# DVE and ACT in written order from tile 72 on, in a fused attention and feed-forward kernel

## The chip, the cores and the metric

The kernel runs on one core of one Trainium2 chip. The metric is the device time of one execution in microseconds; the time before is the median of three runs, 1441.31 us (1440.77 to 1443.91).

## The reference

Attention runs over 8 batches of 8 heads, 576 positions, 64 numbers each, in float32. A score counts if it is at least the row's maximum less tau; softmax goes over the scores that are left. The result is laid out as 4608 tokens of 512 numbers and goes through a feed-forward network (FFN) with 2048 hidden numbers and softplus between its two products. What is computed, cut to its core:

```python
scores = scale * np.matmul(q, k.transpose(0, 1, 3, 2))
thresh = np.max(scores, axis=-1, keepdims=True) - tau
scores = np.where(scores >= thresh, scores, -1000000000.0)
attn = np.exp(scores - np.max(scores, axis=-1, keepdims=True))
attn = attn / (np.sum(attn, axis=-1, keepdims=True) + 1e-09)
x = np.matmul(attn, v).transpose(0, 2, 1, 3).reshape(B * S, H * D)
h = x @ w_in
g = np.maximum(h, 0.0) + np.log1p(np.exp(-np.abs(h)))
out = g @ w_out
```

## The kernel before

**Attention.** The work is cut into 32 units, a batch and a pair of heads each, and a unit into 9 tiles of 128 rows (the fifth tile holds the last 64 rows of both heads): 288 tiles. Names carry the unit and the tile, so negm_10_7 is the maximum of tile 7 of unit 10, which is tile 97 of the kernel. Tile 72 is the first of unit 8. Products run on PE in a format that keeps fewer bits, so operands are split into a hi part and a lo part that is what hi leaves over. For a tile, PE computes scores into one of two PSUM banks (s_0 and s_1, L423); DVE reduces them to the negated row maximum (negm, L430) and sets the threshold (thr, L431); ACT takes the exponential into e_all (L435); DVE masks it and sums its rows (L440). PE then transposes the weights, into the score bank that they came from (L471, L474); ACT copies them out as hi (gH, L498, L503, L510) and DVE makes the lo part (gL, and the corrections in gH, both L132). Only when lo is done may the bank take the scores of the tile two places on. PE multiplies the weights with v (pv, L555 to L557); ACT and DVE add the halves into xp (L565, L566). At a unit's end DVE turns the row sums into factors (rs, L571, L572), which go to POOL by way of memory; POOL scales xp (L593), and SP stores it to x_d.

**FFN.** Tokens come in 9 chunks of 512. A chunk's x is loaded in four quarters (xst, SP, L613); ACT makes xh (L127) and POOL xl (L132). PE makes 16 hidden blocks of 12 matmuls (h, L645 to L649), ACT takes softplus of two blocks at a time (st, L667), DVE casts to hi (g0, L129) and POOL makes lo (g1, L132). PE projects in 4 groups of 4 hidden blocks for 4 blocks of tokens (o, L713; o_1_1_0 is chunk 1, group 1, tokens 0); the sum is kept in acc, set by ACT for the first group (L727) and added to by DVE afterwards (L729). Softplus and the exponential need different tables on ACT, so each change of function has an ACT_TABLE_LOAD.

**The order.** Attention and FFN are woven: the tile loop goes through the letters of `PAT = "ThRlefmpfxSvwp"`. T is the transposes of a tile's weights, h the hi copies, R the reduce of the next tile, l the lo parts, e and m exp and mask of the next tile, S the scores of the tile two places on. Each f lets PE take half of the tile's share of FFN matmuls. Each p is a point at which deferred work is written: softplus, casts of g, the adds into acc, copies of transposed q and k. A chunk's x is split while the chunk before it is projected for the last time; the last quarter is written where the last of these projections ends, right ahead of the chunk's first hidden block.

This written order is not the order that runs. Instructions are handed to a scheduler, which sets the order in each engine's queue by priorities and by estimates of when operands are there. Softplus has a raised priority (`SPP = 150`). Each engine then takes its own queue in that order. Four PSUM banks (tag g) go round among h, o, pv and transposed q and k. Two helpers write order down: `behind(i, others)` makes instruction i come after the last of others in a queue without a wait on a semaphore, and is used for a few instructions only.

Chunk 0 to 6 begin with attention still running; the rest of the FFN comes after the last tile, from about 1240 us.

Of the kernel before, what the change touches and what calls it, by code (L numbers as in the profile page):

```python
# [51 lines left out]
NF = 5  # L52
TG = 36
# [6 lines left out]
def tile_kernel(ctx: ExitStack, tc: tile.TileContext, q, k, v, tau, w_in, w_out, out):  # L60
# [62 lines left out]
    def hi_of(eng, out_, in_):  # L123
        if eng is nc.gpsimd:
            eng.tensor_scalar(out=out_, in0=in_, scalar1=1.0, scalar2=1.0, op0=ALU.mult, op1=ALU.mult)
        elif eng is nc.scalar:
            eng.copy(out_, in_)  # L127
        else:
            eng.tensor_copy(out_, in_)  # L129
# [20 lines left out]
    def to_f32(src, want, name, then):  # L150
# [41 lines left out]
        def first():  # L192
            nc.scalar.activation(m, high.bitcast(F32), AF.Abs, scale=2.0 ** 16)
            nc.gpsimd.tensor_scalar(out=m, in0=m, scalar1=W_MAX, scalar2=W_MIN, op0=ALU.min, op1=ALU.max)
            later_(1, lambda: second(0))


        def second(n):
            if n == 0:
                i = nc.vector.tensor_scalar(out=mu, in0=mu, scalar1=3, scalar2=None, op0=ALU.logical_shift_left)  # L200
            elif n == 1:
                i = nc.vector.scalar_tensor_tensor(out=mu, in0=high, scalar=0x80000000, in1=mu,
                                                   op0=ALU.bitwise_and, op1=ALU.bitwise_or)
            else:
                i = nc.vector.scalar_tensor_tensor(out=mu, in0=low, scalar=29, in1=mu,
                                                   op0=ALU.logical_shift_right, op1=ALU.bitwise_or)
# [68 lines left out]
    for b in range(B):  # L275
        for kind in (("one", "two") if b < NSPLIT else ("all",)):
            for hp in range(NPAIR):
# [14 lines left out]
                s.eng = (nc.gpsimd, nc.scalar)[SPA] if b < NSPLIT else nc.gpsimd  # L292
# [58 lines left out]
    def qkT(s, j, n):  # L351
# [13 lines left out]
        if n == 0:  # L365
            s.kT.append(apool.tile([P, S + SR], F32R, tag="kT", name=f"kT_{s.i}_{j}"))
            t = s.kT[j]
            defer(1, lambda: nc.scalar.copy(t[:, SR:S], ps))
# [6 lines left out]
    def queries(s, t0, t1, ps):  # L375

        nc.scalar.activation(t0, ps, AF.Copy, scale=qscale)
# [3 lines left out]
        for i, o in ((slice(0, D), slice(D, P)), (slice(D, P), slice(0, D))):  # L381
            nc.vector.tensor_scalar(out=t1[o], in0=ps[i], scalar1=qscale[i], scalar2=None, op0=ALU.mult)
# [5 lines left out]
    def qkT_rest(s, j, ps):  # L388

        nc.scalar.copy(  # L390
# [3 lines left out]
        if j == 0 and s.kind != "one":  # L394
            for m in range(2):
                nc.scalar.activation(qm[:, 0, m, m * SR:(m + 1) * SR], ps[:, P + m * SR:P + (m + 1) * SR],
                                     AF.Copy, scale=qscale)
# [29 lines left out]
    def row_max(s, t):  # L427
        negm = apool.tile([P, 1], F32, tag="negm", bufs=3, name=f"negm_{s.i}_{t}")
        thr = apool.tile([P, 1], F32, tag="thr", bufs=3, name=f"thr_{s.i}_{t}")
        nc.vector.reduce_max(negm, s.sp[t][:, :, 0:HS], axis=AX.XY, negate=True)  # L430
        nc.vector.tensor_scalar(out=thr, in0=negm, scalar1=-1.0, scalar2=ntau, op0=ALU.mult, op1=ALU.add)  # L431
        s.m[t] = (negm, thr)

    def exps(s, t):
        nc.scalar.activation(e_all[:, s.half[t], :].rearrange("p (h n) -> p h n", h=2), s.sp[t][:, :, 0:HS],  # L435
                             AF.Exp, bias=s.m[t][0], scale=1.0)

    def mask(s, t):
        e2 = e_all[:, s.half[t], :].rearrange("p (h n) -> p h n", h=2)
        masked.append(nc.vector.scalar_tensor_tensor(  # L440
# [52 lines left out]
    def weights_hi(s, t):  # L493
        main, rest = s.sp[t]
        for g, c0, s0, n in s.place[t]:
            h = group(s, g)[0]
            h = h.bitcast(F32) if s.whole else h
            nc.scalar.copy(h[:, 0:NC, c0:c0 + n], main[:, :, s0:s0 + n])  # L498
        both = rests(s, t)
        if len(both) == 2 and not s.whole:  # L500

            (g, c0, _, n), = s.place[both[0][0]]
            nc.scalar.copy(group(s, g)[0][:, NC, c0:c0 + 2 * n].rearrange("p (k n) -> p k n", k=2),  # L503
                           rest.unsqueeze(1).to_broadcast([P, 2, n]))
            return
        for x, rows, up, down in both:
            for g, c0, s0, n in s.place[x]:
                h = group(s, g)[0][:, NC, c0:c0 + n]
                if not s.whole:
                    nc.scalar.copy(h[up], rest[rows, s0:s0 + n])  # L510
                elif len(both) == 2:
                    nc.scalar.activation(h.bitcast(F32), rest, AF.Copy, scale=side[:, s.half[x]:s.half[x] + 1])  # L512
                else:
                    nc.scalar.copy(h[up].bitcast(F32), rest[rows, s0:s0 + n])
                    nc.gpsimd.memset(h[down].bitcast(F32), 0.0)

    def weights_lo(s, t):
# [3 lines left out]
        for g, c0, s0, n in s.place[t]:  # L521
            h, l = group(s, g)
            lo_of(nc.vector, l[:, :, c0:c0 + n], main[:, :, s0:s0 + n], h[:, 0:NC, c0:c0 + n])
        for x, rows, up, down in rests(s, t):
            for g, c0, s0, n in s.place[x]:
                h = group(s, g)[0]
                lo_of(nc.vector, h[down, NC, c0:c0 + n], rest[rows, s0:s0 + n], h[up, NC, c0:c0 + n])
# [14 lines left out]
    def values(s, g):  # L542
# [5 lines left out]
        if s.whole:  # L548
            slow.append([lambda c=c: nc.tensor.matmul(o[0:D, 0:n], s.vn[:, 5 * j + c, :], h[:, c, 0:n].bitcast(F32),  # L549
                                                      start=(c == 0), stop=(c == NC)) for c in range(NC + 1)])  # L550
            ends.append(lambda: nc.scalar.copy(s.xp[j * D:(j + 1) * D, x0:x0 + n], o[0:D, 0:n]))  # L551
# [8 lines left out]
    def values_out(s, g, o):  # L560
# [4 lines left out]
        nc.scalar.copy(xs, o[move, 0:n])  # L565
        nc.vector.tensor_tensor(out=xs, in0=o[keep, 0:n], in1=xs, op=ALU.add)  # L566

    def row_scales(s):
        nt = len(s.tiles)
        s.rs = apool.tile([P, 9], F32, tag="rs", name=f"rs_{s.i}")  # L570
        nc.vector.tensor_scalar(out=s.rs[:, 0:nt], in0=s.sums[:, 0:nt], scalar1=1e-9, scalar2=None, op0=ALU.add)  # L571
        nc.vector.reciprocal(s.rs[:, 0:nt], s.rs[:, 0:nt])  # L572
# [6 lines left out]
    def row_scales_out(s, ps):  # L579
        nt, n = len(s.tiles), s.n  # L580
        rt = apool.tile([P, S], F32, tag="R", bufs=1, name=f"rt_{s.i}")[0:9, 0:P]
        nc.scalar.copy(rt[0:nt, :], ps[0:nt, 0:P])
# [33 lines left out]
    def split_x(u, cc):  # L616
# [6 lines left out]
        hi_of(nc.scalar, u.h[cc], st)  # L623
# [36 lines left out]
    def softplus(u, full):  # L660
# [3 lines left out]
        with tc.high_priority(SPP):  # L664
            for fc, bank in reversed(full):
                t = fpool.tile([P, TC], F32, tag="st", bufs=NST, name=f"st_{u.n}_{fc}")
                i = nc.scalar.activation(t, bank, AF.Softplus).ins  # L667
# [16 lines left out]
    def parts_of(u, fc, t):  # L684
# [10 lines left out]
        hi_of(nc.vector if u.n else nc.scalar, gh, t)  # L695
# [25 lines left out]
    def project_out(u, qt, tb, o):  # L721
# [4 lines left out]
        if qt == 0:  # L726
            nc.scalar.copy(a, o)  # L727
        else:
            nc.vector.tensor_tensor(out=a, in0=o, in1=a, op=ALU.add)  # L729
# [78 lines left out]
    now = {"p": 0}  # L808
# [114 lines left out]
    eng, u0.eng, u0.eng_lo = u0.eng, nc.scalar, nc.vector  # L923
# [21 lines left out]
    for g, (cur, t) in enumerate(tiles):  # L945
        t9 = cur.tiles.index(t) + 1
# [73 lines left out]
```

## Time and profile before

| | |
|---|---|
| median of 3 runs | 1441.31 us (1440.77 to 1443.91) |
| the profiled execution | 1442.01 us |
| its span, first to last instruction | 1440.2 us |
| mean granted clock of PE | 1.000 |
| PE busy | 1392.3 us, 97% of the span |
| DVE busy | 990.8 us, 69% |
| ACT busy | 850.9 us, 59% |
| POOL busy | 591.0 us, 41% |
| DMA | 189.93 MB, mean 132 GB/s |

Rows of a time line read: start, length, engine, line, operation, out<-in, shapes, count; in brackets the idle time just before on that engine and what ended it. PE rows overlap: a matmul of 512 columns is shown about 0.4 us long, while the next one starts sooner than that. A row of a group reads: line, engine, operation and shapes, count, then busy time and the mean in ns, then the engine's idle time ahead of the group and what ended most of it.

### The profile page before, as it was taken

What the parts mean: (1) busy time and instruction counts of PE and PEld (TensorE: products, weight loads), DVE (VectorE), ACT (ScalarE), POOL (GpSimd) and SP (SyncE); (2) the same over time, 40 slices, a digit from 0 to 9 for tenths busy, and PEclk for the clock granted to TensorE, in tenths of its full rate; (3) what the DMA queues carried; (4) which work ended last, traced back from release to release, by engine and by line L of the source; (5) the groups of instructions that cost most, each with busy time, mean ns of one, the idle gap of its engine ahead of it and who ended that gap; (6) DMA issues with size and microseconds to landing.
All of it is one profiled execution on the core that took longest, in us unless ns stands there. A gap on an engine that the chain in (4) does not pass through costs nothing.

```text
span 1440.2 us, 23512 instructions
## 1 busy us (share of the span) xinstructions
PE 1392.3 (97%) x7860; PEld 1160.7 (81%) x7860; DVE 990.8 (69%) x2211; ACT 850.9 (59%) x1615; POOL 591.0 (41%) x619
## 2 busy tenths in 40 slices
PE   6887899999999999999999999999999999999998
PEld 5555688788888888888888888888888888788886
DVE  6888688787777777777777777777777777402112
ACT  5776777667666576667666665757666765311010
POOL 3676666543334333344334333444334431324221
PEclk9999999999999999999999999999999999999999
DMA  5767766445334534345433533454344532333321
GB/s 156 220 190 206 228 200 184 127 122 160 98 102 119 137 110 124 117 136 152 118 109 107 149 109 99 126 145 121 114 119 139 150 95 83 105 123 126 121 85 44
DMA packets 131208, 189.93 MB, mean 132 GB/s; under 512 B 35312, under 2 KB 86800, under 8 KB 131088
## 3 DMA queue, kind: packets, MB, share of 16 engines
q1 hardware_dynamic: 131088, 188.43, 44.8%
q8 instruction: 63, 1.03, 0.3%
q14 instruction: 57, 0.47, 0.1%
HBM read 140.51 MB, written 27.41 MB: 117 GB/s over the span
## 4 chain that ended last, share of the span: by engine, by line
PE 80%; DVE 8%; ACT 4%; issue 4%; POOL 2%; DMA 1%; SPq 1%; POOLq 0%; DVEq 0%; ACTq 0%
PE o L713 24%; PE s L423 11%; PE h L645 9%; PE h L647 9%; PE h L649 8%; PE s L474 7%; PE pv L555 3%; PE pv L556 3%; DVE e_all L440 2%; PE tr L364 2%; DVE negm L430 1%; ACT L667 1%; PE pv L549 1%; ACT st L667 1%; PE s L471 1%
## 5 line engine op out<-in xcount | busy, mean ns | idle before, releaser
L713 PE MATMUL o<-wo_o,g 128*128 128x512 f32 x1728 | 449.8, 400 | 1.1 <-POOL g L132 1.1
L713 PEld LDWEIGHTS o<-wo_o,g 128*128 128x128 f32 x1728 | 313.4, 188 | 59.9 <-POOL g L132 2.1
L132 POOL TENSOR_TENSOR g<-st,g 128x512 fp32r<-128x512 f32 x144 | 191.5, 1347 | 194.0 <-DVE g L129 180.0
L440 DVE SCALAR_TENSOR_TENSOR e_all<-s,thr,e_all 128x576 f32<-128x576 f32 x288 | 234.1, 815 | 48.8 <-ACT e_all L435 45.3
L430 DVE TENSOR_REDUCE negm<-s 128x1 f32<-128x576 f32 x288 | 216.9, 753 | 37.7 <-PE s L423 30.8
L435 ACT ACTIVATE e_all<-s,negm 128x576 f32<-128x576 f32 x288 | 215.6, 749 | 37.8 <-DVE negm L430 18.6
L645 PE MATMUL h<-xh,wi 128*128 128x512 f32 x576 | 231.3, 402 | 2.1 <-ACT xp L551 0.8
L647 PE MATMUL h<-xl,wi 128*128 128x512 f32 x576 | 232.2, 403 | 0.7 <-POOL xl L132 0.7
L649 PE MATMUL h<-xh,wi 128*128 128x512 f32 x576 | 229.7, 399 | 0.0
L498 ACT CAST gH<-s 128x512 fp32r<-128x512 f32 (+1 forms) x270 | 144.8, 549 | 133.8 <-PE s L474 130.7
L132 DVE TENSOR_TENSOR gL<-s,gH 128x512 fp32r<-128x512 f32 (+1 forms) x270 | 168.9, 634 | 58.1 <-ACT gH L498 31.7
L423 PE MATMUL s<-kT,qT 128*128 128x288 f32 x1024 | 193.0, 310 | 7.8 <-ACT gH L512 2.0
L423 PEld LDWEIGHTS s<-kT,qT 128*128 128x128 f32 x1024 | 148.2, 190 | 29.1 <-issue 9.6
L129 DVE CAST g<-st 128x512 fp32r<-128x512 f32 x128 | 63.0, 529 | 147.9 <-ACT st L667 147.4
L474 PE MATMUL s<-identr,e_all 128*128 128x128 f32 x1008 | 153.6, 275 | 4.0 <-DVE e_all L440 3.9
L667 ACT ACTIVATE st<-h 128x512 f32<-128x512 f32 x144 | 78.3, 596 | 115.6 <-PE h L649 115.1
L474 PEld LDWEIGHTS s<-identr,e_all 128*128 128x128 f32 x1008 | 115.0, 140 | 20.1 <-DVE e_all L440 12.5
L645 PEld LDWEIGHTS h<-xh,wi 128*128 128x128 f32 x576 | 108.4, 188 | 25.7 <-ACT xh L127 1.3
L647 PEld LDWEIGHTS h<-xl,wi 128*128 128x128 f32 x576 | 108.4, 188 | 22.3 <-POOL xl L132 1.4
L649 PEld LDWEIGHTS h<-xh,wi 128*128 128x128 f32 x576 | 108.3, 188 | 22.0
L555 PE MATMUL pv<-gH,vt 128*128 128x256 f32 (+1 forms) x432 | 118.8, 297 | 0.4 <-ACT gH L498 0.4
L556 PE MATMUL pv<-gL,vt 128*128 128x256 f32 (+1 forms) x432 | 118.8, 296 | 0.0
(103 smaller groups left out, 1911.2 us busy)
## 6 DMA issues: line engine op xcount, KB each, us to landing
wi<-wi_d SPq DMA_DIRECT2D x144, 512.0 KB
qT<-qT SPq DMA_DIRECT2D x124, 128.0 KB
R<-r_d SPq DMA_DIRECT2D x64, 144.0 KB
kn<-in_k_dram SPq DMA_DIRECT2D x32, 256.0 KB
qn<-in_q_dram SPq DMA_DIRECT2D x32, 256.0 KB
vn<-in_v_dram SPq DMA_DIRECT2D x32, 256.0 KB
wc_i<-in_moe_w_in_dram SPq DMA_DIRECT2D x16, 512.0 KB
wi_d<-wc_i SPq DMA_DIRECT2D x32, 256.0 KB
```

What stands on the lines that cost most here:

```text
L132: eng.tensor_tensor(out=out_, in0=in_, in1=hi.bitcast(F32), op=ALU.subtract)
L423: i = nc.tensor.matmul(sp[:, hf, 0:HS], lhs, s.kT[j][:, k0 + hf * HS:k0 + (hf + 1) * HS], start=(m == 0), stop=(m == len(parts) - 1))
L430: nc.vector.reduce_max(negm, s.sp[t][:, :, 0:HS], axis=AX.XY, negate=True)
L435: nc.scalar.activation(e_all[:, s.half[t], :].rearrange("p (h n) -> p h n", h=2), s.sp[t][:, :, 0:HS], AF.Exp, bias=s.m[t][0], scale=1.0)
L440: masked.append(nc.vector.scalar_tensor_tensor(out=e2, in0=s.sp[t][:, :, 0:HS], scalar=s.m.pop(t)[1], in1=e2, op0=ALU.is_ge, op1=ALU.mult, ...
L474: nc.tensor.matmul(main[:, c, :], e[:, c0:c0 + P], ident, is_transpose=True, start=True, stop=True)
L555: nc.tensor.matmul(o[:, 0:n], vt[:, c, :], h[:, c, 0:n], start=(c == 0), stop=False)
L556: nc.tensor.matmul(o[:, 0:n], vt[:, c, :], l[:, c, 0:n], start=False, stop=False)
L645: nc.tensor.matmul(h, wi[:, 0, cc, :], u.h[cc], start=(cc == 0), stop=False)
L647: nc.tensor.matmul(h, wi[:, 0, cc, :], u.l[cc], start=False, stop=False)
L649: nc.tensor.matmul(h, wi[:, 1, cc, :], u.h[cc], start=False, stop=(cc == NCC - 1))
L713: nc.tensor.matmul(o, u.g[fc][m // 2][:, sl], wo[fc][:, m % 2, :], start=(n == 0), stop=(n == 3 * QF - 1))
```

## The change

A class `Queue` stands in for DVE (`vec`) and for ACT (`act`) wherever the kernel writes an instruction to them. From tile 72 on, and through all that follows the last tile, it puts each instruction behind the one written before it on the same engine. What is written, and where, stays as it was, and so do the tiles and the buffers. PE, POOL and SP are still ordered by the scheduler, whose estimates see the new order of the other two.

```diff
+TQ = 72
...
+    now = {"p": 0, "tile": 0}
...
+    class Queue:
+
+        def __init__(self, eng):
+            self.eng, self.last = eng, []
+
+        def __getattr__(self, name):
+            def call(*args, **kwargs):
+                i = getattr(self.eng, name)(*args, **kwargs)
+                if now["tile"] >= TQ:
+                    behind(i, self.last)
+                    self.last = [i]
+                return i
+            return call
+
+    vec = Queue(nc.vector)
+    act = Queue(nc.scalar)
...
-        nc.vector.reduce_max(negm, s.sp[t][:, :, 0:HS], axis=AX.XY, negate=True)
+        vec.reduce_max(negm, s.sp[t][:, :, 0:HS], axis=AX.XY, negate=True)
...
-            nc.vector.tensor_tensor(out=a, in0=o, in1=a, op=ALU.add)
+            vec.tensor_tensor(out=a, in0=o, in1=a, op=ALU.add)
...
     for g, (cur, t) in enumerate(tiles):
+        now["tile"] = g
```

Every other `nc.vector` and `nc.scalar` of the loop is replaced in the same way. In the changed kernel all instructions of DVE and ACT carry one line, L156, that of the call in `Queue`.

DVE's queue at the seam of units 10 and 11, before; s_1 is a score bank, acc_1_0 the sum of chunk 1:

```order
L729 TENSOR_TENSOR acc_1_0_4271<-o_1_1_0_4647,acc_1_0_4271 128x512
L440 SCALAR_TENSOR_TENSOR e_all_141,sums_10_4307<-s_1_143,thr_10_7_4690,e_all_141 128x576
L430 TENSOR_REDUCE negm_10_8_4741<-s_0_142 128x1
L431 TENSOR_SCALAR thr_10_8_4742<-negm_10_8_4741,ntau_85 128x1
L132 TENSOR_TENSOR gL_10_3_4739<-s_1_143,gH_10_3_4738 128x4x128
L440 SCALAR_TENSOR_TENSOR e_all_141,sums_10_4307<-s_0_142,thr_10_8_4742,e_all_141 128x576
L571 TENSOR_SCALAR rs_10_4801<-sums_10_4307 128x9
L572 RECIPROCAL rs_10_4801<-rs_10_4801 128x9
L566 TENSOR_TENSOR xp_10_4481<-pv_10_2_4754,xp_10_4481 64x320
L430 TENSOR_REDUCE negm_11_0_4778<-s_1_143 128x1
L729 TENSOR_TENSOR acc_1_0_4271<-o_1_1_1_4706,acc_1_0_4271 128x512
L431 TENSOR_SCALAR thr_11_0_4779<-negm_11_0_4778,ntau_85 128x1
```

The same queue at the same place in the changed kernel:

```order
L156 SCALAR_TENSOR_TENSOR e_all_141,sums_10_4307<-s_1_143,thr_10_7_4690,e_all_141 128x576
L156 TENSOR_TENSOR acc_1_0_4271<-o_1_1_0_4647,acc_1_0_4271 128x512
L156 TENSOR_REDUCE negm_10_8_4741<-s_0_142 128x1
L156 TENSOR_SCALAR thr_10_8_4742<-negm_10_8_4741,ntau_85 128x1
L156 TENSOR_TENSOR gL_10_3_4739<-s_1_143,gH_10_3_4738 128x4x128
L156 SCALAR_TENSOR_TENSOR e_all_141,sums_10_4307<-s_0_142,thr_10_8_4742,e_all_141 128x576
L156 TENSOR_TENSOR xp_10_4481<-pv_10_2_4754,xp_10_4481 64x320
L156 TENSOR_REDUCE negm_11_0_4778<-s_1_143 128x1
L156 TENSOR_SCALAR thr_11_0_4779<-negm_11_0_4778,ntau_85 128x1
L156 TENSOR_TENSOR gL_10_3_4739<-s_0_142,gH_10_3_4738 128x4x128
L156 TENSOR_TENSOR gH_10_3_4738<-s_0_142,gH_10_3_4738 64x128 x2
L156 SCALAR_TENSOR_TENSOR e_all_141,sums_11_4764<-s_1_143,thr_11_0_4779,e_all_141 128x576
```

The add of o_1_1_0 has changed places with the mask of tile 10_7. The add of o_1_1_1 and the two instructions for rs_10 have gone behind the mask of tile 11_0, which is the last row here; they are the next three, and the reduce of tile 11_1 follows them.

ACT's queue ahead of chunk 2, before; xst_2_3 is the last quarter of that chunk's x, and PE reads it in unit 13:

```order
L390 CAST kT_13_0_5466<-tr_13_0_2_5517 128x2x64
L396 ACTIVATE qm_107<-tr_13_0_2_5517,qscale_88 128x64 x2
L377 ACTIVATE qT0_13_0_5525<-tr_13_0_1_5520,qscale_88 128x512
L127 CAST xh_2_2_5620<-xst_2_3_5564 128x512
L498 CAST gH_12_2_5478<-s_1_143 128x4x128
L435 ACTIVATE e_all_141<-s_0_142,negm_12_6_5549 128x576
```

The same queue in the changed kernel, where that instruction now stands:

```order
L156 CAST gH_12_3_5656<-s_0_142 128x4x128
L156 CAST gH_12_3_5656<-s_0_142 128x256
L156 ACTIVATE e_all_141<-s_1_143,negm_13_0_5698 128x576
L156 CAST xh_2_2_5620<-xst_2_3_5564 128x512
L156 CAST kT_13_1_5635<-tr_13_1_2_5732 128x2x64
L156 CAST gH_13_0_5757<-s_1_143 128x4x128
```

The cast of the last quarter has moved from ahead of the exp of tile 12_6 to behind that of tile 13_0. On POOL its lo part moved along, to behind the first split of q for unit 14 (q2_14_0). On PE the one matmul of h_2_0 that reads the last quarter's lo part has gone behind the transpose of tr_13_1_2 and one score matmul.

ACT's queue in unit 13, the first of chunk 2, before:

```order
L503 CAST gH_13_0_5757<-s_0_142 128x256
L667 ACT_TABLE_LOAD
L667 ACTIVATE st_2_1_5821<-h_2_1_5769 128x512
L667 ACTIVATE st_2_0_5823<-h_2_0_5715 128x512
L435 ACT_TABLE_LOAD
L435 ACTIVATE e_all_141<-s_1_143,negm_13_2_5803 128x576
L582 COPY rt_12_5848<-rT_12_5831 9x128
L435 ACTIVATE e_all_141<-s_0_142,negm_13_3_5861 128x576
```

And in the changed kernel:

```order
L156 CAST gH_13_0_5757<-s_0_142 128x256
L156 ACTIVATE e_all_141<-s_1_143,negm_13_2_5803 128x576
L156 ACT_TABLE_LOAD
L156 ACTIVATE st_2_1_5821<-h_2_1_5769 128x512
L156 ACTIVATE st_2_0_5823<-h_2_0_5715 128x512
L156 COPY rt_12_5848<-rT_12_5831 9x128
L156 CAST gH_13_1_5858<-s_1_143 128x4x128
L156 ACT_TABLE_LOAD
L156 ACTIVATE e_all_141<-s_0_142,negm_13_3_5861 128x576
```

The pair of softplus with its table load has changed places with the exp of tile 13_2, and the exp of tile 13_3 has come behind the hi copy of tile 13_1. Two more pairs of the unit, ahead of the exps of tiles 13_4 and 13_6, move in the same way. The number of instructions is the same on every engine, and so is that of table loads. In the first units of the other chunks the rows change as in unit 13; in the three units behind it the pairs of softplus stay where they were.

More of the change, by code (lines that the diff above doesn't have):

```diff
@@ L564, in values_out @@
         xs = s.xp[keep, x0:x0 + n]
-        nc.scalar.copy(xs, o[move, 0:n])
-        nc.vector.tensor_tensor(out=xs, in0=o[keep, 0:n], in1=xs, op=ALU.add)
+        act.copy(xs, o[move, 0:n])
+        vec.tensor_tensor(out=xs, in0=o[keep, 0:n], in1=xs, op=ALU.add)
     def row_scales(s):
@@ L666, in softplus @@
                 t = fpool.tile([P, TC], F32, tag="st", bufs=NST, name=f"st_{u.n}_{fc}")
-                i = nc.scalar.activation(t, bank, AF.Softplus).ins
+                i = act.activation(t, bank, AF.Softplus).ins
                 if last_ is not None:
@@ L807, in tile_kernel @@
     later = []
-    now = {"p": 0}
     def defer(n, f):
```

58 lines of the change are left out of this document (29 added, 29 removed).

## The prediction

> **What bounds the kernel now.** I read the page's engine totals first, then the busy time by stretches of the span, then the groups by line, and last the time line of PE, DVE and ACT around PE's waits.
>
> ```profile
> PE 1392.3 (97%) x7860; PEld 1160.7 (81%) x7860; DVE 990.8 (69%) x2211; ACT 850.9 (59%) x1615; POOL 591.0 (41%) x619
> PE   6887899999999999999999999999999999999998
> ```
>
> PE has work for 97% of the span, and the slices show that what it lacks lies almost wholly in the first fifth, which the change leaves as it is. The stretches (columns: PE, PEld, DVE, ACT and POOL busy, clock, DMA share) say how much is left where the change acts, from tile 72, about 297 us:
>
> ```profile
> 297.00:1240.00 943.00, 937.64 (x5564) 808.52 (x5562) 720.91 (x1651) 619.30 (x1147) 357.80 (x370) 1.00 0.42 120
> 1240.00:1440.20 200.20, 194.82 (x840) 157.31 (x839) 34.88 (x63) 29.24 (x51) 57.47 (x43) 1.00 0.35 108
> ```
>
> In those 943 us PE is idle for 943.00 - 937.64 = 5.4 us by the records. DVE is busy 76% and ACT 66%: neither is a bound, and their order can only matter through PE's few waits. Records of waits start after the overlapped end of the last matmul, so I measure a wait by how far two matmuls start apart, against their undisturbed distance. The groups by line name the wait that is worth most:
>
> ```profile
> L474 PE MATMUL s<-identr,e_all 128*128 128x128 f32 x1008 | 153.6, 275 | 4.0 <-DVE e_all L440 3.9
> L713 PE MATMUL o<-wo_o,g 128*128 128x512 f32 x1728 | 449.8, 400 | 1.1 <-POOL g L132 1.1
> ```
>
> The transposes of the weights wait 3.9 us for the mask. The time line shows where, on PE, at the seam of units 10 and 11; the later rows are the last place of the same kind:
>
> ```profile
> 401.40 0.46 PE L364 MATMUL tr<-identr,k 128*128 128x128 f32 x4
> 401.69 0.51 PE L364 MATMUL tr<-identr,q 128*128 128x128 f32 x4
> 402.03 0.77 PE L423 MATMUL s<-kT,qT 128*128 128x288 f32 x4
> 402.64 0.40 PE L713 MATMUL o<-wo_o,g 128*128 128x512 f32 x1
> 403.37 0.66 PE L474 MATMUL s<-identr,e_all 128*128 128x128 f32 x4 [0.34 <-DVE e_all L440]
> ...
> 407.34 3.00 PE L713 MATMUL o<-wo_o,g 128*128 128x512 f32 x12
> 410.18 0.22 PE L356 MATMUL tr<-identr,k 128*128 128x128 f32 x1
> 410.47 0.76 PE L423 MATMUL s<-kT,qT 128*128 128x288 f32 x4
> ...
> 1190.92 0.66 PE L474 MATMUL s<-identr,e_all 128*128 128x128 f32 x4 [0.33 <-DVE e_all L440]
> ```
>
> Twelve o matmuls and the step to the next instruction take 410.18 - 407.34 = 2.84 us, 0.235 each. The transposes of 403.37 start 0.73 after the o of 402.64, so they lose 0.73 - 0.235 = 0.5 us. At a third of a microsecond of recorded idle each, 3.9 us are 11 to 12 such places; I count 11 in PE's time line, at two seams of every four units. A second, unrecorded loss follows 7 us later: after one transpose (0.29 / 4 = 0.07 each, from the row of 401.40) the scores start 0.29 later, so 0.22 is lost; this too comes 11 times.
>
> DVE's rows at the two places show why:
>
> ```profile
> 401.27 0.59 DVE L132 TENSOR_TENSOR gH<-s,gH 64x128 fp32r<-64x128 f32 x2
> 401.89 0.69 DVE L729 TENSOR_TENSOR acc<-o,acc 128x512 f32<-128x512 f32 x1
> 402.49 0.81 DVE L440 SCALAR_TENSOR_TENSOR e_all<-s,thr,e_all 128x576 f32<-128x576 f32 x1
> 403.23 0.75 DVE L430 TENSOR_REDUCE negm<-s 128x1 f32<-128x576 f32 x1
> ...
> 407.52 0.76 DVE L430 TENSOR_REDUCE negm<-s 128x1 f32<-128x576 f32 x1
> 408.31 0.69 DVE L729 TENSOR_TENSOR acc<-o,acc 128x512 f32<-128x512 f32 x1
> 409.04 0.68 DVE L132 TENSOR_TENSOR gL<-s,gH 128x512 fp32r<-128x512 f32 x1
> 409.74 0.59 DVE L132 TENSOR_TENSOR gH<-s,gH 64x128 fp32r<-64x128 f32 x2
> 411.27 0.76 DVE L430 TENSOR_REDUCE negm<-s 128x1 f32<-128x576 f32 x1
> ```
>
> At each place an add of the FFN into acc, which PE does not need soon, stands ahead of what PE waits for: ahead of the mask at 402.49, and ahead of the gL and gH at 409.04, the last readers of the score bank that the scores of 410.47 overwrite.
>
> ACT around the same places, with a softplus between its two table loads ahead of the first:
>
> ```profile
> 395.60 1.28 ACT L667 ACT_TABLE_LOAD   x1
> 396.89 1.09 ACT L667 ACTIVATE st<-h 128x512 f32<-128x512 f32 x2
> 398.60 0.59 ACT L498 CAST gH<-s 128x512 fp32r<-128x512 f32 x1 [0.18 <-PE s L474]
> 399.48 1.28 ACT L435 ACT_TABLE_LOAD   x1
> 400.78 0.74 ACT L435 ACTIVATE e_all<-s,negm 128x576 f32<-128x576 f32 x1
> 404.54 0.75 ACT L435 ACTIVATE e_all<-s,negm 128x576 f32<-128x576 f32 x1
> ...
> 412.43 0.75 ACT L435 ACTIVATE e_all<-s,negm 128x576 f32<-128x576 f32 x1
> ```
>
> **The change part by part. The mask.** In the written order the add stands behind the mask. The mask then starts when gH ends, about 401.86, and ends at 402.67; PE, which is now given one more o first, wants it at 402.64 + 2 x 0.235 = 403.11. So 0.44 us are to spare and the whole 0.5 goes: 11 x 0.5 = 5.5 us. The add now stands ahead of the reduce of 403.23 instead, but the mask has left its place 0.6 earlier, so the reduce starts when it did. Its exp stands at 404.54 behind a hi copy, 0.56 after the reduce ends, so that is covered.
>
> **The lo parts.** With the add gone from 408.31, gL follows the hi copy and ends, with gH, about 0.6 us earlier; the scores want the bank 0.5 earlier (the gain above) and no longer wait: 11 x 0.22 = 2.4 us. What is late next is the reduce of 411.27: behind it now stand the add (0.69) and the two small row-scale instructions, about 0.4 together. Counted from PE's scores it starts 0.4 later, and its exp, which stood at 412.43 behind a hi copy, 0.40 after the reduce's end, has just that much cover. I take nothing, with 0.2 x 11 = 2.2 us as the bad end.
>
> **The first x split of a chunk.** These rows are ACT, POOL and PE at the start of chunk 2:
>
> ```profile
> 474.60 0.62 ACT L127 CAST xh<-xst 128x512 fp32r<-128x512 f32 x1 [1.60 <-DMA xst<-x_d]
> 487.27 0.76 ACT L435 ACTIVATE e_all<-s,negm 128x576 f32<-128x576 f32 x1
> ...
> 475.30 1.29 POOL L132 TENSOR_TENSOR xl<-xst,xh 128x512 fp32r<-128x512 f32 x1 [1.93 <-ACT xh L127]
> 482.70 0.46 POOL L125 TENSOR_SCALAR q<-qn 128x320 fp32r<-128x320 f32 x1 [4.74 <-PE s L474]
> 483.24 0.88 POOL L132 TENSOR_TENSOR q<-qn,q 128x320 fp32r<-128x320 f32 x1
> 489.43 0.68 POOL L125 TENSOR_SCALAR k<-kn 128x576 fp32r<-128x576 f32 x1 [5.31 <-PE tr L356]
> ...
> 488.89 0.39 PE L647 MATMUL h<-xl,wi 128*128 128x512 f32 x1
> 489.12 0.22 PE L356 MATMUL tr<-identr,k 128*128 128x128 f32 x1
> 489.38 0.76 PE L423 MATMUL s<-kT,qT 128*128 128x288 f32 x4
> ```
>
> Now the last xl is done at 476.59, 12 us before the matmul of 488.89 reads it. In the written order its xh stands behind the exp that starts at 487.27. It starts about 487.9, ends 488.55, and the xl runs on POOL from 488.63 to 489.92. PE has put one transpose and one score matmul ahead of the reader and wants it at about 489.3: a new wait of some 0.65 us. The old wait at this place, 489.38 - 489.12 - 0.07 = 0.2, is again an add ahead of gL, and goes. Six chunk starts lie behind tile 72 with attention still running (0 to 1 up to 5 to 6); the old wait I count at five. That makes 6 x 0.65 - 5 x 0.2 = +2.9 us. The bounds of the new wait are 0 (the POOL queue is empty and exp is earlier) and 2.0 (POOL is still at the two q rows ahead of it, 0.46 + 0.88 more): 0 to 12 us.
>
> **Softplus in the first unit of a chunk.** Three pairs per chunk move behind an exp, 18 in all, with the table loads around them. ACT has run this very order before, at the seam of units 10 and 11, in the first rows quoted of it. Both loads, the pair, the hi copies and the exp fit between 395.60 and 401.52, and the mask behind them was held by the add alone. Cost: zero, with 0.44 us of cover at the transposes. A load is followed by its user 1.29 after its start, so a switch costs the 1.28 of its row. The Trainium skill, "ScalarE: Activation LUTs", section "What ACT_TABLE_LOAD costs", has the same load at about 1283 ns but adds a drain of about 1380 ns to every switch. These rows show no such gap; by the page's price the exp behind the second load would end 2.8 us later at each of the 18 places, an estimate of some 40 us lost, and the trace decides against it, so it gets no chance.
>
> **The end.** The groups' 1.1 us of o waiting for POOL's g is the first projection after attention; its softplus waits for PE's own h, not for an order, so most stays. In the last unit an add leaves the place ahead of gL, too. I take -0.5 us, with -1.0 and +0.5 as ends. In unit 8, where the new order begins, more rows change places than at a seam; I take 0, with one wait of the mask's size, 0.5, to both sides.
>
> **Sum.** -5.5 - 2.4 + 2.9 - 0.5 = -5.5 us. The profiled execution took 1442.01 us (span 1440.2), 0.7 above the median of 1441.31; the sum is 1436.5 against the one and 1435.8 against the other, which is what is asked. A measurement of this kernel can tell about 0.2% from no change, 2.9 us.
>
> **The rivals.** *The same waits under other names.* PE is 99.4% busy in the stretch, and each tile still runs through hi, lo, scores, reduce, exp and mask. If reduce behind add and row scales makes exp late (2.2 us) and half of the mask's gain is lost to the next late thing (2.75 us), the sum is -0.6: 1440.7. For it: everything on DVE is as long as before, and DVE is busy 76% of the time. Against it: the covers worked out above, 0.4 to 0.5 us at each place. Chance 0.18.
>
> *No wait at the chunk start.* If the xl comes in time, 2.9 becomes -1.0: 1435.8 - 3.9 = 1431.9. For it: POOL is idle there before 489.43 but for the two q rows. Against it: exp, xh and xl are a chain of 0.76 + 0.62 + 1.29 us behind a row at 487.27. Chance 0.12.
>
> *Slower: softplus holds up exp in the first unit.* A softplus that ACT must take in its place also holds what is written behind it, the hi copy and the next exp, when PE's h is late. Its place is the 18 moved pairs. The scheduler had them ahead of an exp; now the exp behind them can come later by up to the pair's 1.09, less 0.44 of cover: 0.65 each, 11.7 us, and 1435.8 + 11.7 = 1447.5. It decides from 5.5 / 18 = 0.3 us a place. For it: reduce also stands behind the casts of g there, which wait for softplus, so that two engines stand in line. Against it: the same order at 395.60 cost nothing but the add. Chance 0.17.
>
> *The order does nothing*, since DVE and ACT wait anyway: excluded where I looked, as the add does change places with the mask; it is within the first rival.
>
> **How the numbers follow.** The forecast has 0.53 and gives 1435.8. Its own range is 1431 to 1440, from the ends of the chunk start and of the reduce. The range that holds 8 in 10 reaches down to 1430.5, past the second rival, and up to 1444, between the first rival and the third, which leaves most of the third out. Faster by over 0.2% means below 1438.4: most of the forecast (0.49) and the second rival, 0.61. Within 0.2%: the first rival and the forecast's upper end, 0.21. Slower: the third rival and a chunk start at its bad end, 0.18.
>
> **What would show it.** Right: no recorded wait of the weights' transposes for the mask at the seams of units 10 and 11, and scores 0.07 after the single transpose there; a wait of PE for xl of 0.4 to 0.9 us in the first hidden block of each chunk; PE idle of about 3 us between 297 and 1240. Wrong: a chunk start that costs 2 us, transposes that wait for the mask in units 9, 13, 17, or a late reduce at the seams.

## The result, and the profile after

The changed kernel takes 1431.93 us (median of 6 runs, 1428.68 to 1434.79) against 1441.17 us before (6 runs): a ratio of 0.9932, 95% interval 0.992 to 0.9945. It is faster by 9.2 us. The forecast was 1435.8, faster by 5.5; 1431.93 is where the forecast put the second rival, but the trace shows that it got there by another way.

The engine totals of the page and, below them, the stretch from 297 to 1240 us of the changed kernel (columns as before):

```profile
PE 1386.3 (97%) x7860; PEld 1166.4 (82%) x7860; DVE 988.3 (69%) x2211; ACT 847.9 (59%) x1615; POOL 588.0 (41%) x619
```
```profile
297.00:1240.00 943.00, 936.36 (x5592) 818.96 (x5591) 722.12 (x1652) 618.98 (x1151) 359.24 (x373) 1.00 0.42 121
```

PE's recorded idle time in the stretch has not fallen: 943.00 - 936.36 = 6.6 us, where it was 5.4. Yet 5592 matmuls fall into it, and 5564 did before. Busy time is no measure here, since a matmul's record overlaps the next one's; the count of matmuls in equal time is.

PE's groups by line; the last column names what it waited for:

```profile
L732 PE MATMUL o<-wo_o,g 128*128 128x512 f32 x1728 | 446.0, 400 | 0.4 <-POOL g L133 0.4
L666 PE MATMUL h<-xl,wi 128*128 128x512 f32 x576 | 231.9, 403 | 4.6 <-POOL xl L133 4.6
L442 PE MATMUL s<-kT,qT 128*128 128x288 f32 x1024 | 194.3, 311 | 7.4 <-ACT gH L156 3.8 <-DVE gL L156 1.4 <-DVE qT L156 0.2
L493 PE MATMUL s<-identr,e_all 128*128 128x128 f32 x1008 | 151.4, 272 | 0.0
```

The transposes' wait for the mask, 3.9 us before, is 0.0. The hidden blocks' wait for xl is new. The seam of units 10 and 11, on PE and then on DVE (here and below, rows of small instructions such as thr are left out):

```profile
399.40 0.46 PE L383 MATMUL tr<-identr,k 128*128 128x128 f32 x4
399.69 0.51 PE L383 MATMUL tr<-identr,q 128*128 128x128 f32 x4
400.28 0.76 PE L442 MATMUL s<-kT,qT 128*128 128x288 f32 x4
400.88 0.63 PE L732 MATMUL o<-wo_o,g 128*128 128x512 f32 x2
401.35 0.60 PE L493 MATMUL s<-identr,e_all 128*128 128x128 f32 x4
...
407.86 0.22 PE L375 MATMUL tr<-identr,k 128*128 128x128 f32 x1
407.92 0.76 PE L442 MATMUL s<-kT,qT 128*128 128x288 f32 x4
```
```profile
399.54 0.59 DVE L156 TENSOR_TENSOR gH<-s,gH 64x128 fp32r<-64x128 f32 x2
400.16 0.82 DVE L156 SCALAR_TENSOR_TENSOR e_all<-s,thr,e_all 128x576 f32<-128x576 f32 x1
400.91 0.69 DVE L156 TENSOR_TENSOR acc<-o,acc 128x512 f32<-128x512 f32 x1
401.51 0.75 DVE L156 TENSOR_REDUCE negm<-s 128x1 f32<-128x576 f32 x1
```

The add stands behind the mask, the transposes start two o matmuls after the scores without a gap (401.35 - 400.88 = 0.47, two times 0.235), and the scores of 407.92 start 0.06 after the single transpose, where it was 0.29. Both old waits are gone. But the scores of 400.28 start 0.59 after the four transposes of q, where they started 0.34 after them (402.03 - 401.69): a wait of 0.25 that was not there. They wait for the gH of 399.54, which ends at 400.13, the last reader of their bank.

The start of chunk 2, on ACT, POOL and PE:

```profile
483.46 0.76 ACT L156 ACTIVATE e_all<-s,negm 128x576 f32<-128x576 f32 x1
484.10 0.63 ACT L156 CAST xh<-xst 128x512 fp32r<-128x512 f32 x1
```
```profile
484.81 1.28 POOL L133 TENSOR_TENSOR xl<-xst,xh 128x512 fp32r<-128x512 f32 x1 [3.02 <-ACT xh L156]
```
```profile
485.12 0.22 PE L375 MATMUL tr<-identr,k 128*128 128x128 f32 x1
485.18 0.35 PE L442 MATMUL s<-kT,qT 128*128 128x288 f32 x1
486.14 0.50 PE L666 MATMUL h<-xl,wi 128*128 128x512 f32 x1 [0.62 <-POOL xl L133]
```

The chain exp, xh, xl runs as the prediction laid it out; PE starts the reader 0.96 after a score matmul that takes about 0.13.

To compare whole traces I take the distance between the starts of each two successive matmuls, less the short distance (the 5th percentile) of a matmul of that kind and shape, and sum it from the first reduce of unit 8 to the last matmul. The short distances alone, the ideal part, come to 1004.7 us before and 1003.8 changed; the difference comes from 1 ns in that of a score matmul (128 and 127 ns). What lies above the ideal part, in us, with the number of places over 30 ns, by what PE came from and what it started:

| | before | changed |
|---|---|---|
| o, then transposes of weights (waits for the mask) | 5.81 (13) | 0 |
| transposes of k, then scores (waits for lo) | 3.79 (21) | 0 |
| transposes of q, then scores (waits for lo) | 0 | 4.48 (17) |
| scores, then h (waits for xl) | 0 | 5.00 (6) |
| transposes of weights among themselves | 64.85 (768) | 62.03 (768) |
| scores, transposes of q, h or pv, then transposes of weights | 2.94 (27) | 0 |
| from the first reduce of unit 8 to the last matmul | 1142.05 | 1133.78 |

Most of row 5 is in both kernels; only the difference counts. From unit 8 on the run is shorter by 8.3 us. The rest of the difference of the two profiled executions, 1.2 us, lies ahead of unit 8, where the order is the same; in the kernels below that leave the first units as they are, unit 8's first reduce starts anywhere between 290.0 and 293.3 us, so that is spread from run to run. All figures of waits below are of one profiled execution of each kernel, summed in this manner.

### The profile page after: what moved, and what is told of

Read it like the earlier page. It is cut to its first block, busy times and chain, and to the rows that moved or that the text cites. A ratio compares the mean times of both kernels' runs of the same rounds, so it can differ in the third digit from the quotient of the medians.

```text
span 1430.8 us, 23585 instructions
## 1 busy us (share of the span) xinstructions
PE 1386.3 (97%) x7860; PEld 1166.4 (82%) x7860; DVE 988.3 (69%) x2211; ACT 847.9 (59%) x1615; POOL 588.0 (41%) x619
## 4 chain that ended last, share of the span: by engine, by line
PE 82%; DVE 4%; DMA 3%; issue 3%; POOL 3%; ACT 2%; SPq 2%; POOLq 0%; ACTq 0%; DVEq 0%
PE o L732 25%; PE s L442 11%; PE h L666 9%; PE h L668 8%; PE h L664 8%; PE s L493 7%; PE pv L574 4%; PE pv L575 3%; PE tr L383 2%; PE pv L568 2%; DVE e_all L156 1%; DMA qn<-in_q_dram 1%; PE pv L576 1%; PE s L490 1%; DVE negm L156 1%
## 5 line engine op out<-in xcount | busy, mean ns | idle before, releaser
L156 ACT CAST gH<-s 128x512 fp32r<-128x512 f32 (+2 forms) x432 | 179.6, 467 | 144.2 <-PE s L493 118.2
L156 DVE SCALAR_TENSOR_TENSOR e_all<-s,thr,e_all 128x576 f32<-128x576 f32 x288 | 235.2, 817 | 40.7 <-ACT e_all L156 36.4
L156 ACT ACTIVATE e_all<-s,negm 128x576 f32<-128x576 f32 x288 | 216.2, 751 | 32.6 <-PE tr L490 15.5
L156 DVE TENSOR_REDUCE negm<-s 128x1 f32<-128x576 f32 x288 | 215.6, 748 | 26.1 <-PE s L442 22.5
L156 DVE TENSOR_TENSOR gL<-s,gH 128x512 fp32r<-128x512 f32 (+1 forms) x270 | 169.1, 635 | 47.7 <-ACT gH L156 39.5
L156 DVE CAST g<-st 128x512 fp32r<-128x512 f32 x128 | 57.7, 492 | 170.6 <-ACT st L156 170.6
L156 ACT ACTIVATE st<-h 128x512 f32<-128x512 f32 x144 | 78.3, 596 | 112.4 <-PE h L668 111.8
L493 PEld LDWEIGHTS s<-identr,e_all 128*128 128x128 f32 x1008 | 119.3, 140 | 10.6 <-DVE e_all L156 2.6
```

The costliest lines, as they stand in the source:

```text
L156: i = getattr(self.eng, name)(*args, **kwargs)
L493: nc.tensor.matmul(main[:, c, :], e[:, c0:c0 + P], ident, is_transpose=True, start=True, stop=True)
```

## The experiments

**Theory and rival.** Theory A: the gain is DVE's, because the adds into acc leave the place ahead of mask and lo. Theory B: it is ACT's, because softplus stands behind exp. Four kernels tell them apart: each engine's order alone, the adds alone, and the changed kernel without the adds.

*ACT alone.* DVE's stand-in passes instructions on without an order.

```diff
-    vec = Queue(nc.vector)
+    vec = Queue(nc.vector, on=False)
...
-                if now["tile"] >= TQ:
+                if self.on and now["tile"] >= TQ:
```

> Only ACT takes the written order; DVE stays with the scheduler, which puts the adds into acc ahead of the mask again. Theory A (the gain is DVE's: the adds leave the place ahead of mask and lo): both old waits stay, about 0.5 and 0.23 us at the seams, and the wait for the last xl of 0.83 us at six chunk starts comes on top: about 1445 us, 1443 to 1447. Theory B (the gain comes from ACT's order, softplus behind exp): about as the changed kernel, 1431 to 1435 us.

Measured: 1437.89 us, ratio 0.9969 (0.9953 to 0.9985). Neither theory's number. Both old waits are there as A says (5.56 us for the mask, 2.61 for lo) and so is the new one for xl (six times 0.73), but the part from unit 8 on is still 4.1 us shorter than before. None of the 27 short waits in row 6 of the table is left. (The profiled execution took 1434.91 us, 3 below the median.)

*DVE alone*, made in the same way with `act`:

> Only DVE takes the written order; on ACT the cast of the last x quarter is early again. Theory A: no transposes wait for the mask, and the 6 x 0.83 us for xl are gone: 1432 - 5 = 1427 us, 1425 to 1430. Theory B: the gain is lost with ACT's order: 1438 to 1442 us. The wait of the scores for lo of about 0.25 us a unit that the changed kernel has would stay if DVE's casts of g cause it, and go if ACT's order of softplus causes it.

Measured: 1440.17 us, ratio 0.9995 (0.9986 to 1.0005). The time is theory B's, the waits are A's: those for the mask at the seams and those for lo behind the single transposes are gone. The gain goes elsewhere. The scores wait 2.85 us behind the transposes of q, at 11 places, with ACT's order left to the scheduler. And ACT's cast of x, early again, waits for its DMA ahead of other work: ACT is idle 2.40 us in unit 8, where PE then loses 2.3 us at the mask, and 1.95 and 2.14 us at two chunk starts, where PE loses 0.55 and 0.74 us behind pv. From unit 8 on the kernel is 2.6 us shorter than before. By its time alone it does not speak for A; the next two kernels do.

*The adds alone*, in the kernel before:

```diff
-            nc.vector.tensor_tensor(out=a, in0=o, in1=a, op=ALU.add)
+            i = nc.vector.tensor_tensor(out=a, in0=o, in1=a, op=ALU.add)
+            if now["tile"] >= TQ:
+                behind(i, masked)
```

> The kernel before, with one thing of the change alone: from tile 72 on each add into acc is put behind the last mask written; everything else is left to the scheduler. Theory A: the waits for the mask (5.8 us by the trace) and the scores' wait behind the single transpose (3.8 us) go, nothing new at the chunk starts: 1441 - 9 = 1432 us, 1430 to 1434. Theory B: 1439 to 1442 us.

Measured: 1433.2 us, ratio 0.9938 (0.9924 to 0.9953), as A says. From unit 8 on it takes 1134.23 us, 7.8 less than before. This one line of order brings nearly all that the whole change brings. One wait for the mask is new: 1.94 us in unit 8, where ACT's cast of x stands ahead of an exp and waits 2.11 us for its DMA.

*The changed kernel with the adds left free* (`nc.vector` in that line, and nothing else):

> The changed kernel, with the adds into acc alone given back to the scheduler, which puts them ahead of the mask at the seams again. Theory A: the two old waits are back beside the new ones: 1432 + 9 = 1441 us, 1438 to 1443. Theory B: 1431 to 1434 us.

Measured: 1438.91 us, ratio 0.9985 (0.9975 to 0.9995), as A says. The waits for the mask (3.32 us) and for lo behind the single transpose (2.66) are back, beside those for xl and for lo behind the transposes of q (4.40).

PE's weight loads show the same in one row each: the loads of the weights to be transposed, and their idle time for the mask, in the kernel before, the changed one, ACT alone, the adds alone and the adds free:

```profile
L474 PEld LDWEIGHTS s<-identr,e_all 128*128 128x128 f32 x1008 | 115.0, 140 | 20.1 <-DVE e_all L440 12.5 <-issue 0.4
```
```profile
L493 PEld LDWEIGHTS s<-identr,e_all 128*128 128x128 f32 x1008 | 119.3, 140 | 10.6 <-DVE e_all L156 2.6 <-issue 0.9
```
```profile
L493 PEld LDWEIGHTS s<-identr,e_all 128*128 128x128 f32 x1008 | 116.0, 140 | 18.4 <-DVE e_all L156 11.2 <-issue 0.4
```
```profile
L475 PEld LDWEIGHTS s<-identr,e_all 128*128 128x128 f32 x1008 | 116.4, 140 | 11.7 <-DVE e_all L441 5.4 <-issue 0.4
```
```profile
L493 PEld LDWEIGHTS s<-identr,e_all 128*128 128x128 f32 x1008 | 117.5, 140 | 18.0 <-DVE e_all L156 9.7 <-issue 0.4
```

12.5 us fall to 2.6 with the whole change and to 5.4 with the adds alone; with the adds in their old place they stay near 10 whatever ACT does. So A holds for the larger part, as far as the adds go: it is their place that brings the gain, and not DVE's whole order. B holds for a smaller one. Of the short waits in row 6 of the table, 18 of about 0.1 us stand in units 9, 13, 17, 21, 25 and 29, three in each: the first units of the chunks, where three pairs of softplus stood ahead of an exp. All 18 are there with the adds alone and none with ACT alone.

**The chunk starts.** *The x split free:* ACT's casts of x are given back to the scheduler, which puts the last one early again.

```diff
-        hi_of(act, u.h[cc], st)
+        nc.scalar.copy(u.h[cc], st)
```

> The changed kernel, with ACT's casts of a chunk's x (xh) alone given back to the scheduler, which puts the last of them some 12 us earlier again. Theory: the wait of PE for xl, 0.83 us at six chunk starts in the changed kernel, is caused by that cast's place alone: 1432 - 5 = 1427 us, 1425 to 1429. Rival: an xh that is early stands ahead of hi copies while its DMA is still out, as the run with the adds alone shows once (0.85 us at one chunk start): then half is lost again, 1429 to 1431.

Measured: 1435.57 us, ratio 0.9956 (0.9939 to 0.9973), slower than the changed kernel. The wait for xl is gone, but the rival was right and too small. At one chunk start, on ACT, DVE and PE:

```profile
631.30 0.62 ACT L642 CAST xh<-xst 128x512 fp32r<-128x512 f32 x1 [4.15 <-DMA xst<-x_d]
631.82 0.58 ACT L156 CAST gH<-s 128x512 fp32r<-128x512 f32 x1
```
```profile
632.43 0.69 DVE L156 TENSOR_TENSOR gL<-s,gH 128x512 fp32r<-128x512 f32 x1 [4.61 <-ACT gH L156]
```
```profile
633.18 1.16 PE L442 MATMUL s<-kT,qT 128*128 128x288 f32 x4 [2.58 <-DVE gL L156]
```

A cast that the scheduler had put ahead of the landing of its data left ACT idle for 4.15 us; the hi copy, lo and the scores waited in line behind it. In unit 8 the same cast stands ahead of an exp (1.51 us for the DMA), and PE loses 1.5 us at the mask.

*The split in the middle:* the last quarter stays in the written order but is written halfway through the last projection, not behind it.

```diff
-    def project(u, qt, tb):
+    def project(u, qt, tb, mid=None):
...
+            if mid and n == 5:
+                mid()
...
-            yield from project(u, it[2], it[3])
-            if it[4] and it[3] == u.T // P - 1:
-                for cc in range(it[3] * per, NCC):
-                    split_x(nx, cc)
+            last_x = it[4] and it[3] == u.T // P - 1
+            yield from project(u, it[2], it[3], (lambda: split_x(nx, NCC - 1)) if last_x else None)
```

> The changed kernel, with one thing written elsewhere: the last quarter of the next chunk's x is split in the middle of the last projection and not behind it, so that in the written order its cast stands behind the exp of the tile before (12_8 and not 13_0), some 3 us earlier, when its DMA has landed. Theory: the wait for xl at six chunk starts (0.83 us each) goes, and no hi copy waits behind a cast whose data are out: 1432 - 5 = 1427 us, 1425.5 to 1428.5. Rival: the early cast pushes hi copies and exps back, as giving the casts to the scheduler did: 1430 to 1436.

Measured: 1428.44 us, ratio 0.9906 (0.9886 to 0.9926). The cast now runs behind the exp of the tile before, and the same places read, on ACT, POOL and PE:

```profile
480.90 0.77 ACT L156 ACTIVATE e_all<-s,negm 128x576 f32<-128x576 f32 x1
481.54 0.64 ACT L156 CAST xh<-xst 128x512 fp32r<-128x512 f32 x1
```
```profile
482.82 1.28 POOL L133 TENSOR_TENSOR xl<-xst,xh 128x512 fp32r<-128x512 f32 x1
```
```profile
485.96 0.39 PE L666 MATMUL h<-xl,wi 128*128 128x512 f32 x1
486.19 0.22 PE L375 MATMUL tr<-identr,k 128*128 128x128 f32 x1
```

The xl is done at 484.10 and PE reads it at 485.96 without a wait. The time is within the theory's range. From unit 8 on the kernel takes 1128.80 us, 5.0 less than the changed one: the whole of the 6 x 0.83.

**The scores' new wait for lo.** *The casts late:* DVE's casts of g are written one point later (`HD = (1, 2)` for `(1, 1)`).

> The changed kernel, with DVE's casts of g written one point later, behind the next mask and not ahead of the next reduce. Theory: the new wait of the scores for lo (17 places of 0.26 us) ends a chain of hi, exp, table load, softplus pair, casts, reduce and lo; without the casts in it the wait goes: 1432 - 4.4 = 1427.6 us, 1426 to 1430. Rival: the wait comes from ACT's part of the chain alone, exp behind hi, and stays: 1431 to 1433. A later g could also make the projections wait for POOL: 1433 or more.

Measured: 1455.59 us, ratio 1.01 (1.007 to 1.013). The wait at 17 places went, and 24 us came. PE's projections in that kernel:

```profile
L732 PE MATMUL o<-wo_o,g 128*128 128x512 f32 x1728 | 448.0, 401 | 4.4 <-POOL g L133 4.4
```

They wait 4.4 us for POOL's g. Behind the mask the casts also push the reduce back: scores, then transposes, lose 7.93 us at 38 places, 0.2 us each. From unit 8 on the kernel takes 1156.25 us, 22.5 more than the changed one, in an execution that was 5.2 us above the median.

*The last two in one,* but with the x split free and not in the middle:

> Both of the last two in one kernel. If the two waits are apart, 1432 - 5 - 4.4 = 1422.6 us, 1421 to 1426. If PE only meets the next wait sooner, 1426 to 1430.

Measured: 1451.05 us, ratio 1.0063 (1.0038 to 1.0087): the casts decide. 

*The add into xp late:* `defer(1, lambda: vec.tensor_tensor(...))` around DVE's add in `values_out`, and *both,* with the split in the middle:

> The changed kernel, with DVE's add into xp (0.48 us) written one point later, behind the next mask and not between the casts of g and the reduce. If the scores wait for lo because that whole chain on DVE is 0.25 us too long, a chain shorter by 0.48 ends the wait at 17 places: 1432 - 4.4 = 1427.6 us, 1426 to 1430. Rival: what is put behind the mask makes the next reduce late, as the casts did, or a PSUM bank comes free late: 1432 to 1440.

> Both of these: 1432 - 5 - 4.4 = 1422.6 us if each ends its own wait; as the first alone, 1427, if the second brings nothing.

Measured: 1445.64 us, ratio 1.0028 (1.0016 to 1.004), and 1441.66 us, 0.9995 (0.9983 to 1.0008). The rival's direction, but no clean test: on PE the scheduler now puts transposes of the weights among those of q and k, and PE loses 6.1 us between the two and 3.89 us at the single transposes again. One DVE instruction written later has changed the order of another engine.

*One between:* so the test has to leave DVE and ACT as they are. The wait's chain begins on PE. PE, ACT and DVE of the changed kernel ahead of the wait at 400.28:

```profile
390.89 0.76 PE L442 MATMUL s<-kT,qT 128*128 128x288 f32 x4
391.49 0.39 PE L666 MATMUL h<-xl,wi 128*128 128x512 f32 x1
391.72 0.40 PE L668 MATMUL h<-xh,wi 128*128 128x512 f32 x1
391.96 0.60 PE L493 MATMUL s<-identr,e_all 128*128 128x128 f32 x4
```
```profile
392.60 0.59 ACT L156 CAST gH<-s 128x512 fp32r<-128x512 f32 x1 [0.57 <-PE s L493]
393.08 0.75 ACT L156 ACTIVATE e_all<-s,negm 128x576 f32<-128x576 f32 x1
393.85 1.28 ACT L156 ACT_TABLE_LOAD   x1
395.14 1.08 ACT L156 ACTIVATE st<-h 128x512 f32<-128x512 f32 x2
```
```profile
396.26 1.36 DVE L156 CAST g<-st 128x512 fp32r<-128x512 f32 x2 [1.57 <-ACT st L156]
397.54 0.48 DVE L156 TENSOR_TENSOR xp<-pv,xp 64x320 f32<-64x320 f32 x1
397.94 0.74 DVE L156 TENSOR_REDUCE negm<-s 128x1 f32<-128x576 f32 x1
398.85 0.68 DVE L156 TENSOR_TENSOR gL<-s,gH 128x512 fp32r<-128x512 f32 x1
```

From the transposes of 391.96 to the gH that ends at 400.13 each step begins as the last one ends: hi, exp, table load, the softplus pair, its casts, xp, reduce, lo. In the kernel before one h matmul stands between the scores and these transposes, not two:

```profile
392.85 0.76 PE L423 MATMUL s<-kT,qT 128*128 128x288 f32 x4
393.45 0.40 PE L647 MATMUL h<-xl,wi 128*128 128x512 f32 x1
393.68 0.63 PE L474 MATMUL s<-identr,e_all 128*128 128x128 f32 x4
```

There they start 0.83 after the scores, here 1.07: the chain begins 0.24 later, and the scores at its end wait 0.25. The last kernel has the split in the middle, and holds all FFN matmuls but the first behind these transposes:

```diff
+        turned[:] = [i] if t == 5 and now["tile"] >= TQ else []
+        since[0] = 0
...
+    def after_T(i):
+        since[0] += 1
+        if since[0] > 1:
+            behind(i, turned)
...
-            nc.tensor.matmul(h, wi[:, 0, cc, :], u.h[cc], start=(cc == 0), stop=False)
+            after_T(nc.tensor.matmul(h, wi[:, 0, cc, :], u.h[cc], start=(cc == 0), stop=False))
```

and so for the other FFN matmuls; `i` is the last transpose.

> The kernel with the split in the middle, with one thing more: the transposes of a unit's sixth tile stand behind one FFN matmul on PE and no more (the scheduler puts two or three there; it put one there in the kernel before), and as it comes out, those of the eighth tile too. Theory: the scores' wait of 0.26 us at 17 places ends a chain that those transposes begin (hi, exp, table load, softplus pair, casts of g, reduce, lo); begun one matmul, 0.235 us, sooner, the wait goes, and DVE and ACT stay in the same order: 1428.4 - 4.4 = 1424 us, 1422.5 to 1426. Rival 1: the chain is not what holds the scores, and the wait stays: 1428.4. Rival 2: the transposes now wait for the mask instead, up to 0.25 us at each: 1427 to 1432.

Measured: 1426.66 us, ratio 0.9899 (0.9883 to 0.9915). Behind the transposes of q the scores' loss falls at all 17 places, from 4.47 us to 1.82, 0.26 to 0.11 each. So the chain, begun sooner, causes most of the wait. A part stays: at the seam of units 10 and 11 the chain itself took 8.28 us here (390.93 to 399.21) and 8.17 in the changed kernel (391.96 to 400.13), and why it is longer is not shown. At one place in the first unit of each of the six chunks the transposes now wait 0.2 us for the mask (1.24 us), as the second rival had it. From unit 8 on it is 1.1 us faster than with the split alone. The time is a little above the theory's range, and the times alone do not tell the two kernels apart.

**The start of the order.** *From tile 36* (`TQ = 36`):

> The changed kernel with the written order from tile 36 on and not 72. The theory of adds gives nothing here: chunk 0's projections begin at tile 44, so a few adds lie between, up to 1 us. PE is short of work there for other reasons. 1431 to 1433 us; more than 2 us either way would say that the order of the first batches matters in itself.

Measured: 1454.41 us, ratio 1.0089 (1.0068 to 1.0109). A miss by 22 us. From unit 8 on it is much as the changed kernel (1135.42 us, 1133.78 there); unit 8 begins at 312.1 us and not at 292.0. PE's scores from 140 us to the start of unit 8, in this kernel and in the changed one:

```profile
L442 PE MATMUL s<-kT,qT 128*128 128x288 f32 x116 | 23.1, 324 | 13.1 <-DVE gH L156 6.1 <-DVE gL L156 5.0 <-ACT gH L156 0.9
```
```profile
L442 PE MATMUL s<-kT,qT 128*128 128x288 f32 x116 | 21.9, 309 | 3.6 <-ACT gH L156 1.9 <-DVE gL L156 1.4
```

In units 4 to 7 the written order makes the scores wait for lo, 11 us in all by these two releasers. The longest wait, on ACT, DVE and PE, shows what stands ahead of lo:

```profile
262.50 0.68 ACT L156 ACTIVATE ws_o<-wc_o 128x512 f32<-128x512 f32 x1 [5.48 <-DMA wc_o<-in_moe_w_out_dram]
263.91 0.43 DVE L156 TENSOR_SCALAR ws_o<-ws_o 128x512 uint32<-128x512 uint32 x1 [5.76 <-POOL ws_o L213]
267.35 1.33 PE L442 MATMUL s<-kT,qT 128*128 128x288 f32 x4 [3.73 <-DVE gL L156]
```

In these units the weights of the second FFN product are still being loaded and split, by ACT, POOL and DVE in turn (wc_o, wa_o, ws_o). In the written order ACT waits for their DMA, DVE waits for ACT and POOL with the reduce and gL in line behind, and PE waits for gL. A chain of the same kind, from the ws_o that ACT starts at 234.72, costs PE 2.27 and 1.67 us at 239.92 and 242.12. Unit 6, in which both stand, takes 54.3 us from its first reduce to that of unit 7; in the changed kernel, where the scheduler orders this part, it takes 40.6, and from 125 us on DVE waits at most 0.95 us for such a piece. So by the traces most of the 20 us is the price of work that stands in line before its data have landed; no run tried it by itself.

## Why the prediction came out as it did

**The mask and the lo parts: right, and a little small.** Forecast 5.5 and 2.4 us, and 1.0 for the old wait at the chunk starts: 8.9. The table has 5.81 + 3.79 = 9.6. Shown by the adds alone, which bring 7.8 from unit 8 on, and by the adds left free. The late reduce at the seams, 2.2 us as a bad end, cost nothing: rows 1 and 6 are 0 in the changed kernel.

**The chunk start: right in mechanism, 0.83 for 0.65.** PE's reader stood one score matmul and one transpose behind, as forecast, but PE came to it earlier, at about 485.3 where exp, xh and xl end at 486.09. Six places make 5.0 against 3.9. The second rival, that this wait is not there, is wrong, though its time was nearly met.

**The step that failed: "Cost: zero" for softplus, and the extra o as slack.** The prediction took the one FFN matmul more ahead of the seam's transposes for cover, 0.44 us of it, and priced only the wait for the mask. One FFN matmul more also stands ahead of the transposes some 9 us earlier (the h of 391.72), and starts that tile's hi, and with it a chain through both engines, 0.235 us later. Where a pair of softplus lies in that chain, it has no cover at all. It cost 4.5 us at 17 places, which no term of the sum had. The third rival named this line of ACT and DVE, softplus, casts, reduce, but put it in the first units and priced it at 11.7; it came in the first unit of a chunk and the two behind it, one place a unit, and because of PE's order.

**What the sum did not have.** Against the 4.5 lost stand 5.7 us of gain that was not forecast. The short waits of row 6 are 2.9 of it, 1.7 at the 18 places of softplus, which the prediction had at nothing; at 21 of the 27 places the weight loads' rows in the kernel before name the mask as what ended the wait. The transposes among themselves are 2.8, and 2.0 of that lie in the 40 tiles of rows 1 and 6, whose transposes had waited: about 0.05 us a tile more between the four or five of them. So the larger part of these gains is the mask's wait again, in pieces too small to show as idle time in PE's rows, and the forecast's term for it was too small. That the forecast is off by no more than 3.7 is in part luck: a loss of 4.5 and a gain of 5.7, both left out, nearly cancel. The balance against the forecast is -0.7 (mask and lo), +1.1 (chunk starts), +4.5 (scores), +0.5 (the end, below), -5.7 (these two) and -1.2 (ahead of unit 8), -1.5 together. The result is 3.7 below the forecast; the other 2.2 are pieces of 1.0 us or less, the largest of them 1.0 between o matmuls (17.05 to 16.09) and the 1.0 of the ideal part; their causes stay open.

**The end.** Forecast -0.5. The first projection after attention waits 0.6 and not 1.0, but the last pv and the row scales now lose 0.79 and 0.72: nothing is left of it.

**What the prediction said would show it.** The mask's wait at 0.0 and the scores 0.06 after the single transpose came; the wait for xl came. PE idle of about 3 us between 297 and 1240 did not: it is 6.6, in a stretch that does more work. That sign does not measure the gain.

## What to carry to other kernels

When an engine's order is fixed, look for what leaves the critical place, and try that alone: one dependency on the adds into acc brought nearly as much as the order of two whole engines. Work whose result is not needed soon goes behind the instruction that another engine waits for; work that waits for a transfer goes where its data have landed, whether a scheduler or the written order would put it sooner. And follow a moved instruction past its first user: a matmul that is cover for one wait delays the chain that begins behind it.

## What the runs showed of the hardware

A wait that ends while the last matmul still drains leaves no idle time in PE's rows but is seen at the weight loads: 12.5 us of waiting for the mask there, 3.9 in the matmul rows. Busy time of PE went down with the waits (1392.3 to 1386.3 us over the span), so neither busy nor idle time of matmul rows measures the gain. A switch of ACT's table cost 1.29 us again (393.85 to 395.14), with work waiting behind it; the drain that the Trainium skill adds to it ("ScalarE: Activation LUTs", "What ACT_TABLE_LOAD costs") is in none of these rows.
